# Triangular factors turned by VectorE block transposes instead of a trip through DRAM, with the first steps ordered anew

## The chip, the cores and the metric

The kernel runs on one core of one Trainium2 chip. Its metric is the device time of one execution in microseconds; three runs of the kernel before took 694.21 (median), 695.6 and 693.18 us.

Engines are named as in the profile: PE is TensorE (matrix products; PEld its weight loads), DVE is VectorE, ACT is ScalarE, POOL is GpSimd, and SP is the engine that issues most DMAs. Each engine works through its own list of instructions in order and waits where an operand isn't ready.

## The reference

A delta-rule attention layer is followed by a hard-swish MLP. Batch 4, 8 heads, 768 tokens, head width 48:

```python
k_n = k / (np.linalg.norm(k, axis=-1, keepdims=True) + 1e-06)
for t in range(S):
    y[:, :, t] = einsum('bhd,bhde->bhe', q[:, :, t], state)
    v_old = einsum('bhde,bhd->bhe', state, kt)
    state = state + bt * einsum('bhd,bhe->bhde', kt, vt - v_old)
...
x = y.transpose(0, 2, 1, 3).reshape(3072, 384)
h = x @ w_in                      # 384 x 2048
g = h * clip(h + 3, 0, 6) / 6
out = g @ w_out                   # 2048 x 384
```

q, k, v and beta are float32; the two weight matrices arrive as float64.

## The kernel before, in words

**Attention in chunks.** The tokens are cut into 24 chunks ("tiles" t) of 32 tokens; the 4 batches of a chunk fill the 128 partitions (partition = batch, token). Within a chunk the recurrence becomes linear algebra: with L the strictly lower triangular 32x32 matrix of beta-weighted key products of one batch and head, the chunk needs the inverse of (1 + L). There are 4 x 8 = 32 such matrices in a chunk.

- `prep(t)` normalizes the keys (POOL, kb), transposes keys and queries on PE (pt, copied by ACT to KQ), forms the scores (sc), and multiplies them with a mask on VectorE into LB. LB holds two halves for each head: the factor L, and the masked query-key scores.
- `lower(t)` sends the half with L to a DRAM scratch, l_dram, through SP (L446).
- Chunks come in groups: group 0 is chunk 0 alone, groups 1 to 5 have four chunks each, group 6 has three. A group of four has 4 x 32 = 128 matrices. `inverse(g)` loads them from l_dram with one matrix per partition (tile A, 1024 elements each), runs 30 pairs of VectorE instructions (a product pr, L719, and a subtraction from A, L724), sets the diagonal, stores A to x_dram (L730) and loads it back, chunk by chunk, over the L half of LB (L738).
- Group 1 is needed early. `halves_of(1)` does only the two 16x16 diagonal blocks, in 14 pairs (L681, L686), with the same trip out (L671) and back (L693, L700), and `join(t)` fills the remaining block with two sets of small PE products (pi, L633) between VectorE block transposes (L643, L651).
- Chunk 0 uses `product(0)`, a scheme of PE products and 32x32 VectorE transposes, with no DRAM.
- `chain(t)` is the recurrence: state times keys and queries (ks, L775), the right side R on VectorE (L788), the inverse times R on PE (pz, ACT copy Z), the state update (su, L892; VectorE L907), and the chunk's output y (py, yt, ACT copy xT).

**MLP.** Two chunks make a block of 256 tokens. `up` multiplies with w_in (ph, 16 column units of 128; L946). ACT computes relu(ph/6 + 1/2) into t1 (L955, three buffers), and VectorE min(t1, 1) * ph into g (L958). Block 0 is done in halves by chunk, ua and ub. `down` multiplies with w_out (po, L987); from block 2 on, `down_by_seven` does this with seven half-size products on sums of g (L1052; the sums on VectorE, L1038).

**Weights.** Sixteen pieces of 768 KB (w_in eight, w_out eight) are loaded in float64 (L310) and turned to float32: four ACT instructions for the exponent (L335, word `a`), three VectorE instructions (L357, L362, L368, word `c`). Their raw data lie in `spare` and in parts of w_out.

**What sets the order.** The schedule is written by hand. Until the fifth chunk it is the string ORDER: each word advances one generator by a step, and the engines' instruction lists follow from it. `k`, `q`, `v`, `w` issue loads on SP; `pN`, `nN`, `mN`, `bN` are parts of prep of chunk N; `i1`, `i2` are steps of the inverse of group 1 and 2; `x` is product or join; `h` and `y` the chain and its output; `ua`, `ub`, `u` MLP units with their ACT part (`ra`, `rb`, `ru`) and VectorE part (`ga`, `gb`, `gu`). From chunk 5 on a loop over chunks does it: 15 MLP units a chunk, with chain and prep steps at fixed units, and the steps of the next group's inverse as fill from the second chunk of each group. SP allows about eight DMAs in flight: each issue waits for the landing of the eighth before it.

Of the kernel before, what the change touches and what calls it, by code (L numbers as in the profile page):

```python
# [9 lines left out]
FP32 = mybir.dt.float32  # L10
# [5 lines left out]
ALU = mybir.AluOpType  # L16
# [6 lines left out]
k*4 B*4 w s n0 k*2 n0 z*2 s k n0*2 z n0 k z n1 n0*2 q z a*3 p0 m0 k*2 q n1*2 q c k q s c n1 w p0 a  # L23
p0*3 k a k n2 k*2 q z s k*2 q p0 w n1*2 a c n1 p0 s q a p1 x0 n2*2 a n2 s x0 n2 x0*2 k a n2 a*2
n2*2 p1 n2 q*3 a m1 c w k x0*2 c q s k c x0 b0 p1 a q p1 a p2 v x0 c p1 a c x0 c*3 v q x0 n4*2 p2
k x0 p2*2 p1 w b1 a b2 m2 c q n4 q*3 p2 q c*2 p1 v x0 w n4*3 p3 a*2 n4 p2 m3 p3 a*2 q p3 p4 x0 a w
p3 p4 a p2 c p3 q p4 x0 p4*2 a*3 m4 v p3 a k c p4 p3 p4 w c*2 a c x0*2 h0 a c a l1 l2 a c l3 h0 l4
a*2 c y0 i1 k y0 v b3 y0 c*2 k y0 w ua*2 w i1 ra i1*4 ua i1*7 a i1 k i1*7 a i1*2 k v ra i1*2 a ga
i1 h0 i1 ra ua i1 ua i1 ra i1 ga ua ga*2 ra c ga ra k ga h0 ua ra ga k ua n5 a ra v ga ua a ra c
ua v ra i1 ga*2 c a ua h1 ua*2 n5 x1 w ra*2 ua ga i1 x1 ga c x1 v k x1 x2 k x1 n5 ra n5 i1 ga a*2  # L30
h1 x1 c m5 w ua c v h1 ra y1 h1 x3 y1*2 a h1 ga i1 k*2 a v c a*2 h1 y1 ua ra a n5 x2 k h2 y1 k x2
n5 b4 c y1 ga ub*2 ra k ga q k n5 x2 w ub rb n5 a n5 v n5 k rb x2 gb y2 n5*2 gb rb x2 q ub rb n5
h2 ub gb rb i1 q gb p5 gb k p6 s h2 v ub rb k p5 h2 p5 ub x3*2 q y2 q k v b5 b6 x4 x3 gb k n9 q
ub*3 rb w rb*2 gb*2 c a v gb ub y2 ub k y2 h2 rb gb rb gb v rb a*2 v n9 gb h2 x3*2 ub p5 q rb ub c
ub p5 p7 gb y2 ub rb*2 h3 gb*2 c v p6 a k a y2 h3 p8 k y3 p6 k rb gb k n9 u q y3 p7 h3 q k n9 p7
h3 p8*2 a c k q y3*2 p6 c y3 u y3 a p6 c m6 w q u c a ru h3 a n9 gu x4 h3 a u k q ru q k c q*2 a v
k q a u q u gu n9 p5 v c k p6 a p7 w p7 u n9 p6 ru p5 v*2 n9 m7 v b8 a gu u p8 n9 p8 m8 p7 c p8 q
ru p7 n9 s u a p8 u b7 q u l5 a gu k u n9 a u ru n9*2 v c gu q u p9*2 c h4 ru c gu q l6 a p9 c*3 v
x4*2 u l8 ru h4 u p10 gu l7 y4 k m9 m10 y4 p10 q u q p10 q u i2*2 ru i2*4 k gu p10 x4 p10 v x4 p9
i2 p9 i2 q u*2 i2 v i2*2 v i2*2 ru i2*4 k i2*3 gu i2 u h4 i2*2 ru i2*4 p9 h4 p9 p10*2 i2 u*2 k gu  # L40
ru u*2 i2*3 q i2 gu i2*4 k u i2 u i2 ru gu u b10 u i2 ru i2*9 q ru k u gu u l10 e h4 e y4 u i2*2
gu i2*2 k i2 ru i2 l9 i2 q i2 ru i2 u i2 u i2*3 k i2 k b9 k p11 h4 k y4 k*4 e i2 y4 gu e i2*3 u*2
gu y4
# [4 lines left out]
def kernel(  # L48
# [368 lines left out]
    l_dram, x_dram = {}, {}  # L417
# [13 lines left out]
    def scaled(t):  # L431
        needs(("kb", t), *pad(t), *([("bkb", t - NKB)] if t >= NKB else []))
        nc.gpsimd.tensor_tensor(
            out=bkbufs[t % NBKB][:, :, 0:D], in0=kbufs[t % NKB][:, :, 0:D],
            in1=beta_tok[:, t, 0:H].unsqueeze(2).to_broadcast([P, H, D]), op=ALU.mult,
        )
        past.add(("bkb", t))
        yield

    def lower(t, dma=nc.sync):  # L440
        g, i = group(t)
        if g > 0:
            if g not in l_dram:
                l_dram[g] = scratch.tile([size(g), H, P, C], FP32, name=f"l_dram{g}")
                x_dram[g] = scratch.tile([size(g), H, P, C], FP32, name=f"x_dram{g}")
            dma.dma_start(  # L446
                out=l_dram[g][i].rearrange("h p c -> p h c"),
                in_=LBs[t][:].rearrange("p e a j w -> p (e a) j w")[:, :, 0, :],
            )
        past.add(("L", t))  # L450
        yield

    def prep(t, whole=True):
# [36 lines left out]
        for p in range(NP):  # L490
# [12 lines left out]
        LB = work.tile([P, 2, NP, 2, C], FP32, name="LB", bufs=NLB)  # L503
        mb = mbs.pop(t)
        nc.vector.tensor_tensor(  # L505
            out=LB[:].rearrange("p e a j w -> p e (a j w)"), in0=sc[:, :, 0 : NP * 2 * C],
            in1=mb[:].rearrange("p e a j w -> p e (a j w)"), op=ALU.mult,
        )
# [5 lines left out]
        if whole:  # L514
            drain(lower(t))
            yield

    def product(t):
# [7 lines left out]
        LT = LBs[t][:].rearrange("p e a j w -> p (e a) j w")[:, :, 0, :]  # L526
# [88 lines left out]
    def join(t):  # L615
# [6 lines left out]
        LT = LBs[t][:].rearrange("p e a j w -> p (e a) j w")[:, :, 0, :]  # L622
# [41 lines left out]
    def halves_of(g):  # L664

        n = size(g) * H * B
        needs(*(("L", first(g) + i) for i in range(size(g))))
        At = work.tile([128, C + 1, C], FP32, name="A", bufs=1)
        flat = At[0:n].rearrange("p c i -> p (c i)")
        A = flat[:, 0 : C * C]  # L670
        nc.sync.dma_start(  # L671
            out=A, in_=l_dram[g][:].rearrange("t h (b c) i -> (t h b) (c i)", b=B),
        )
# [3 lines left out]
        for j in range(1, HC - 1):  # L677
# [15 lines left out]
        nc.sync.dma_start(  # L693
            out=x_dram[g][:].rearrange("t h (b c) i -> (t h b) (c i)", b=B), in_=A,
        )
        past.add(("out", g))
        for i in range(size(g)):
            yield
            LBv = LBs[first(g) + i][:].rearrange("p e a j w -> p (e a) j w")
            nc.sync.dma_start(out=LBv[:, :, 0, :], in_=x_dram[g][i].rearrange("h p c -> p h c"))  # L700
            past.add(("halves", first(g) + i))
# [631 lines left out]
```

## Time and profile before

| | |
|---|---|
| median of 3 runs | 694.21 us |
| the profiled execution | 691.84 us, span 690.1 us |
| PE busy | 648.2 us (94%) |
| VectorE busy | 440.1 us (64%) |
| ScalarE busy | 239.8 us (35%) |
| mean granted PE clock | 0.975 |
| DMA moved | 45.27 MB |
| l_dram, x_dram transfers | 23 of 128 KB out (2.7 us each), 6 to A (5.1), 6 from A (3.6), 23 of 128 KB back (4.0) |

The profile follows one execution. A line of a timeline has start, duration, engine, source line, operation and operands, and in brackets the idle time before it and what ended that. A line of the table of stretches has the stretch, its length, busy time with the count of instructions for each engine asked for, the mean granted PE clock, the DMA share and GB/s. The chain is the line of work that ended last, followed back from the end.

### The profile page before, as it was taken

What the parts mean: (1) busy time and instruction counts of PE and PEld (TensorE: products, weight loads), DVE (VectorE), ACT (ScalarE), POOL (GpSimd) and SP (SyncE); (2) the same over time, 40 slices, a digit from 0 to 9 for tenths busy, and PEclk for the clock granted to TensorE, in tenths of its full rate; (3) what the DMA queues carried; (4) which work ended last, traced back from release to release, by engine and by line L of the source; (5) the groups of instructions that cost most, each with busy time, mean ns of one, the idle gap of its engine ahead of it and who ended that gap; (6) DMA issues with size and microseconds to landing.
All of it is one profiled execution on the core that took longest, in us unless ns stands there. A gap on an engine that the chain in (4) does not pass through costs nothing.

```text
span 690.1 us, 25473 instructions
## 1 busy us (share of the span) xinstructions
PE 648.2 (94%) x11208; PEld 568.0 (82%) x11208; DVE 440.1 (64%) x1174; ACT 239.8 (35%) x476; POOL 95.2 (14%) x146
## 2 busy tenths in 40 slices
PE   1659799999999999999999999999999999999997
PEld 1548687767678988988988988988988989989997
DVE  5878656788535985834985734984544984445242
ACT  5886558522133223232233232232222132132230
POOL 5440021710401100501100401100000000000000
PEclk9967799999999999999999999999999999999999
DMA  7987746513614126024025122025020014000000
GB/s 163 211 205 212 167 99 145 111 21 92 74 36 97 22 47 91 14 47 95 15 47 77 28 47 64 10 48 82 10 70 2 2 36 59 24 3 1 25 0 24
DMA packets 137999, 45.27 MB, mean 66 GB/s; under 512 B 128192, under 2 KB 131264, under 8 KB 137888
## 3 DMA queue, kind: packets, MB, share of 16 engines
q1 hardware_dynamic: 137632, 43.35, 30.6%
q8 instruction: 88, 1.44, 0.9%
q10 hardware_dynamic: 256, 0.30, 0.2%
q14 instruction: 23, 0.19, 0.1%
HBM read 32.87 MB, written 10.75 MB: 63 GB/s over the span
## 4 chain that ended last, share of the span: by engine, by line
PE 78%; DVE 11%; DMA 6%; issue 2%; ACT 2%; SPq 1%; DVEq 0%
PE ph L946 33%; PE po L1052 23%; PE po L987 6%; PE ks L775 3%; PE pz L796 3%; PE py L796 3%; PE su L892 2%; DVE A L724 2%; PE pt L474 2%; DMA w_out<-in_moe_w_in_dram 2%; PE sc L495 2%; DVE pr L719 2%; DMA spare<-in_moe_w_in_dram 2%; DVE g L1038 1%; ACT spare L335 1%
## 5 line engine op out<-in xcount | busy, mean ns | idle before, releaser
L946 PE MATMUL ph<-xT,w_in 128*128 128x256 f32 (+1 forms) x1248 | 270.7, 370 | 2.7 <-DVE g L958 1.6
L946 PEld LDWEIGHTS ph<-xT,w_in 128*128 128x128 f32 x1248 | 221.2, 193 | 32.1 <-DVE g L958 2.6
L955 ACT ACTIVATE t<-ph,halves 128x256 f32<-128x256 f32 (+1 forms) x208 | 94.8, 457 | 203.8 <-PE ph L946 194.2
L958 DVE SCALAR_TENSOR_TENSOR g<-t,ph 128x256 f32<-128x256 f32 (+1 forms) x208 | 81.7, 397 | 124.6 <-ACT t L955 124.5
L1052 PE MATMUL po<-w_out,g 128*128 128x192 f32 x640 | 113.3, 328 | 0.0
L1052 PEld LDWEIGHTS po<-w_out,g 128*128 128x128 f32 x640 | 103.9, 190 | 0.5
L1052 PE MATMUL po<-spare,g 128*128 128x192 f32 x480 | 84.8, 330 | 0.0
L1052 PEld LDWEIGHTS po<-spare,g 128*128 128x128 f32 x480 | 78.1, 190 | 1.8
L1038 DVE TENSOR_TENSOR g<-g 128x256 f32<-128x256 f32 x160 | 65.5, 463 | 0.5 <-PE po L1052 0.5
L724 DVE TENSOR_TENSOR A<-A,pr 128x30 f32<-128x30 f32 (+19 forms) x150 | 52.1, 348 | 3.5
L335 ACT ACTIVATE spare<-spare,places 128x768 uint16<-128x768 uint16 (+1 forms) x56 | 52.3, 939 | 1.9 <-DMA spare<-in_moe_w_in_dram 1.0
L719 DVE TENSOR_TENSOR pr<-A 128x30 f32<-128x30 f32 (+19 forms) x150 | 50.4, 336 | 3.3
L423 POOL TENSOR_TENSOR mb<-beta_tok,mask 128x256 f32<-128x256 f32 x48 | 35.2, 755 | 78.3 <-DVE LB L505 78.3
L987 PE MATMUL po<-w_out,g 128*128 128x384 f32 x128 | 44.8, 490 | 0.0
L1059 ACT ACTIVATE o<-po 128x192 f32<-128x192 f32 x40 | 13.2, 330 | 88.6 <-PE po L1052 84.3
L458 POOL TENSOR_TENSOR kb<-kf,inv 128x384 f32<-128x384 f32 x24 | 21.8, 910 | 147.0 <-PE pt L474 88.8
L482 ACT ACTIVATE KQ<-pt 128x512 f32<-128x512 f32 x48 | 28.3, 594 | 30.5 <-PE pt L474 29.7
L845 ACT ACTIVATE xT<-yt 128x384 f32<-128x384 f32 x24 | 11.7, 486 | 68.6 <-PE yt L841 68.6
L987 PEld LDWEIGHTS po<-w_out,g 128*128 128x128 f32 x128 | 23.4, 190 | 13.4 <-issue 0.6
L907 DVE TENSOR_TENSOR state<-state,su 128x384 f32<-128x384 f32 x46 | 23.3, 547 | 14.7 <-PE su L892 14.7
L775 PEld LDWEIGHTS ks<-state,KQ 64*64 64x64 f32 x1472 | 24.2, 138 | 6.2 <-issue 5.7
L788 DVE SCALAR_TENSOR_TENSOR y<-ks,parity,y 128x192 f32<-128x192 f32 x46 | 17.0, 410 | 18.4 <-ACT y L812 18.3
(104 smaller groups left out, 570.3 us busy)
## 6 DMA issues: line engine op xcount, KB each, us to landing
kf<-in_k_dram SPq DMA_DIRECT2D x96, 48.0 KB, 2.6
qb<-in_q_dram SPq DMA_DIRECT2D x96, 48.0 KB, 2.9
vf<-in_v_dram SPq DMA_DIRECT2D x96, 48.0 KB, 3.2
out_dram<-o SPq DMA_DIRECT2D x92, 48.0 KB, 1.6
spare<-in_moe_w_in_dram SPq DMA_DIRECT2D x4, 768.0 KB, 7.6
w_out<-in_moe_w_in_dram SPq DMA_DIRECT2D x4, 768.0 KB, 6.9
w_out<-in_moe_w_out_dram SPq DMA_DIRECT2D x4, 768.0 KB, 7.8
spare<-in_moe_w_out_dram SPq DMA_DIRECT2D x4, 768.0 KB, 5.5
```

The costliest lines, as they stand in the source:

```text
L335: nc.scalar.activation(out=z, in_=z if n else d.bitcast(I16)[:, :, :, 3], func=func, bias=places[:, n : n + 1], scale=scale,)
L423: nc.gpsimd.tensor_tensor(out=mb[:, e], in0=beta_tok[:, t, e:H:2].unsqueeze(2).unsqueeze(3).to_broadcast([P, NP, 2, C]), in1=mask2[:].unsq ...
L719: nc.vector.tensor_tensor(out=pv, in0=A[:, j, j + 1 :].unsqueeze(1).to_broadcast([n, j, w]), in1=A[:, 0:j, j].unsqueeze(2).to_broadcast([n ...
L724: nc.vector.tensor_tensor(out=A[:, 0:j, j + 1 :], in0=A[:, 0:j, j + 1 :], in1=pv, op=ALU.subtract)
L775: nc.tensor.matmul(ph[y][c, e, D * p : D * p + D], lhsT=KQ[r, p * B // 2 + b // 2, 2 * y : 2 * y + 2, :].rearrange("k y c -> k (y c)"), rh ...
L796: nc.tensor.matmul(ps[rows(place(b)), D * h : D * h + D], lhsT=m(h)[rows(b)], rhs=z[rows(b), D * h : D * h + D], start=True, stop=True, sk ...
L946: nc.tensor.matmul(ph[:, cols], lhsT=w_in[:, s, f * 128 : (f + 1) * 128], rhs=xT[:, s, cols], start=(s == 0), stop=(s == NKT - 1),)
L955: nc.scalar.activation(out=t1, in_=ph, func=ACTF.Relu, bias=half, scale=1.0 / 6.0)
L958: nc.vector.scalar_tensor_tensor(out=g, in0=t1, scalar=1.0, in1=ph, op0=ALU.min, op1=ALU.mult)
L987: nc.tensor.matmul(pos[c][:], lhsT=gs[blk, f // 2][:, f % 2, c * P : (c + 1) * P], rhs=w_out[:, f, :], start=(f == 0), stop=(f == NFC - 1),)
L1038: nc.vector.tensor_tensor(out=A(f, *out), in0=A(f, *a), in1=A(f, *b), op=op)
L1052: nc.tensor.matmul(ps[n][:], lhsT=A(f - f % 2, *a)[:, f % 2], rhs=b[:, f], start=(f == 0), stop=(f == HF - 1),)
```

## The change

Four edits:

- The factors no longer go through DRAM. prep writes L into a tile of its own, `L` (four chunks), and the scores into a smaller LB, with two VectorE instructions in place of one. `taken(g)` transposes L in 32x32 blocks into A, one matrix per partition, and `given(g)` transposes A back into a tile `X`, which pz, `product` and `join` read. Each is one VectorE instruction of 128x1024; both of its operands step by 32 elements. `lower`, l_dram, x_dram and their DMAs are gone. Chunk 0 writes L directly into its X.
- ORDER is a new string. Up to its end it does the same steps apart from those that no longer exist (the words l1 to l10, four of i1, four of i2).
- ACT writes its part of the hard-swish into g itself, and VectorE finishes it in place; t1 is gone.
- The steps of a last group with three chunks run on all 128 partitions, the rest filled with zeros.

```diff
 ORDER = """
-k*4 B*4 w s n0 k*2 n0 z*2 s k n0*2 z n0 k z n1 n0*2 q z a*3 p0 m0 k*2 q n1*2 q c k q s c n1 w p0 a
+k*3 B k B*3 z n0*3 w z*3 s z q*2 n0 q n0 q v n0 w n0 a p0 a p0 s p0*2 m0 k*2 w p0 a*3 p0 a c a c v
...
 """
...
+    def inverted(g):
+        if g not in Xs:
+            if g >= 2:
+                needs(*(("pz", first(g - 2) + i) for i in range(size(g - 2))))
+            Xs[g] = work.tile([P, GS, H, C], FP32, name="X", bufs=2)
+        return Xs[g]
+
+    def lowers(t):
+        g, i = group(t)
+        if g == 0:
+            return inverted(g)[:, i]
+        if g not in Ls:
+            needs(*([("A", g - 1)] if g >= 2 else []))
+            Ls[g] = work.tile([P, GS, H, C], FP32, name="L", bufs=1)
+            if size(g) < GS:
+                nc.gpsimd.memset(Ls[g][:, size(g) :], 0.0)
+        return Ls[g][:, i]
...
+    def turn(x):
+        return x[:].rearrange("p t h i -> p i (t h)")
+
+    def problems(A):
+        return A.rearrange("p (c i) -> p i c", i=C)
+
+    def taken(g, A):
+        nc.vector.transpose(out=problems(A), in_=turn(Ls[g]))
+        past.add(("A", g))
+
+    def given(g, A):
+        nc.vector.transpose(out=turn(inverted(g)), in_=problems(A))
...
-    def lower(t, dma=nc.sync):
-        g, i = group(t)
-        if g > 0:
...
-            dma.dma_start(
-                out=l_dram[g][i].rearrange("h p c -> p h c"),
-                in_=LBs[t][:].rearrange("p e a j w -> p (e a) j w")[:, :, 0, :],
-            )
...
-        LB = work.tile([P, 2, NP, 2, C], FP32, name="LB", bufs=NLB)
+        LB = work.tile([P, H, C], FP32, name="LB", bufs=NLB)
         mb = mbs.pop(t)
-        nc.vector.tensor_tensor(
-            out=LB[:].rearrange("p e a j w -> p e (a j w)"), in0=sc[:, :, 0 : NP * 2 * C],
-            in1=mb[:].rearrange("p e a j w -> p e (a j w)"), op=ALU.mult,
-        )
+        for j, out in enumerate((lowers(t), LB)):
+            nc.vector.tensor_tensor(
+                out=out.rearrange("p (e a) w -> p e a w", e=2), in0=scv[:, :, :, j, :],
+                in1=mb[:, :, :, j, :], op=ALU.mult,
+            )
...
-        dma.dma_start(
-            out=A.rearrange("p c i -> p (c i)"),
-            in_=l_dram[g][:].rearrange("t h (b c) i -> (t h b) (c i)", b=B),
-        )
+        taken(g, flat)
...
-        back.dma_start(
-            out=x_dram[g][:].rearrange("t h (b c) i -> (t h b) (c i)", b=B),
-            in_=A.rearrange("p c i -> p (c i)"),
-        )
-        past.add(("out", g))
-        for i in range(size(g)):
-            yield
-            LBv = LBs[first(g) + i][:].rearrange("p e a j w -> p (e a) j w")
-            back.dma_start(out=LBv[:, :, 0, :], in_=x_dram[g][i].rearrange("h p c -> p h c"))
-            past.add(("X", first(g) + i))
+        given(g, flat)
+        past.update(("X", first(g) + i) for i in range(size(g)))
...
-        of_heads(pz, lambda b: b, lambda h: LBv[:, he(h), 0, :], R)
+        of_heads(pz, lambda b: b, lambda h: X(t)[:, he(h), :], R)
+        past.add(("pz", t))
...
-                t1 = mlp.tile([128, TB], FP32, name="t1", bufs=3)[:, cols]
-                nc.scalar.activation(out=t1, in_=ph, func=ACTF.Relu, bias=half, scale=1.0 / 6.0)
+                nc.scalar.activation(out=g, in_=ph, func=ACTF.Relu, bias=half, scale=1.0 / 6.0)
...
-                        out=g, in0=t1, scalar=1.0, in1=ph, op0=ALU.min, op1=ALU.mult
+                        out=g, in0=g, scalar=1.0, in1=ph, op0=ALU.min, op1=ALU.mult
```

`halves_of(1)` changes in the same way as `inverse` (shown), with `taken` in place of its load and `given` in place of its store and loads.

In the instruction lists that follow from the new ORDER: on SP the eighth w_in piece is the 43rd transfer instead of the 54th. On PE the first state update su of chunk 0 stands ahead of the first up-projection ph, as do all scores sc of chunks 1 to 4; fifteen up-projections with ks of chunk 1 (fourteen before) stand ahead of the first join product. On ACT all 32 conversion instructions of w_in stand ahead of the last three KQ copies of chunks 3 and 4. On VectorE the 28 factor steps of group 1 stand behind the conversions of w_in, as before, with twelve instead of four hard-swish instructions among them. Group 2's factor steps lie between MLP units 17 and 36 of the u stream; before, between 18 and 36, with the last chain steps of chunk 4 among them.

## The prediction

> **What bounds the kernel now.** I read the page's first two parts, then engine busy time by stretch, the chain, the waits ahead of ScalarE's weight work, and VectorE in one dense stretch. From the page:
>
> ```profile
> span 690.1 us, 25473 instructions
> PE 648.2 (94%) x11208; PEld 568.0 (82%) x11208; DVE 440.1 (64%) x1174; ACT 239.8 (35%) x476; POOL 95.2 (14%) x146
> ...
> PE   1659799999999999999999999999999999999997
> ...
> PEclk9967799999999999999999999999999999999999
> ```
>
> TensorE is full from the sixth slice on. Busy time of PE in stretches of the span (start:end, length, busy, granted clock, DMA share, GB/s):
>
> ```profile
> 40.00:54.40 14.40, 7.64 (x327) 0.58 0.78 201
> 54.40:61.30 6.90, 6.89 (x94) 0.63 0.53 142
> 61.30:72.30 11.00, 9.01 (x248) 1.00 0.88 240
> 72.30:84.00 11.70, 9.45 (x277) 0.56 0.77 151
> 84.00:100.00 16.00, 15.18 (x519) 1.00 0.54 119
> ...
> 230.00:690.00 460.00, 454.81 (x7011) 1.00 0.20 37
> ```
>
> From 230 us on PE lacks 5.2 us, of which 3.6 lie after 650, in the unchanged tail: 1.6 us is all that later stages could give. PE's work before and after is the same, so the time moves by what PE idles, or runs at half clock, before 184 us, and by new stalls later. The chain, in time order (start, length):
>
> ```profile
> 52.53 0.96 DVE w_in L368
> ...
> 61.30 3.56 DMA x_dram<-A
> 64.88 4.55 DMA LB<-x_dram
> ```
>
> The trip back costs 3.56 + 4.55 = 8.1 us. The trip out costs nothing: group 1's factor steps begin at 53.41, right behind that weight conversion, with A issued at 47.95. Up to 52.5 the chain is ScalarE's conversions. Their waits for weights:
>
> ```profile
> 15.76 0.99 ACT L335 ACTIVATE spare<-spare,places 128x768 uint16<-128x768 int16 x1 [0.97 <-DMA spare<-in_moe_w_in_dram]
> 21.33 1.00 ACT L335 ACTIVATE spare<-w_out,places 128x768 uint16<-128x768 int16 x1 [0.23 <-DMA w_out<-in_moe_w_in_dram]
> 26.83 0.99 ACT L335 ACTIVATE spare<-w_out,places 128x768 uint16<-128x768 int16 x1 [1.11 <-DMA w_out<-in_moe_w_in_dram]
> 33.21 1.04 ACT L335 ACTIVATE spare<-w_out,places 128x768 uint16<-128x768 int16 x1 [0.45 <-DMA w_out<-in_moe_w_in_dram]
> ```
>
> Sum 2.76 us. Last, VectorE where a later group is factored, and after it:
>
> ```profile
> 228.00:256.00 28.00, 26.92 (x73) 1.00 0.19 38
> 256.00:268.00 12.00, 8.73 (x29) 1.00 0.25 66
> ```
>
> VectorE has 1.1 us free in 28; PE stalls 0.58 us for it at 255. Behind that, 3.3 us are free in 12.
>
> **What the skill says.** The Trainium skill, "TensorE: Matmul & The Clock Gate", Part 1: the array falls to half clock after an idle window of some 3.4 us and comes back after a busy one. The trace agrees in kind: PE is half idle from 68 to 72, and from 74 to 82 the clock is 0.50. "Vector Engine (DVE) Microarchitecture Reference", section 5.2: about 1.04 ns a column, but near 2.0 when source and destination both hop at every element, up to 2.5 for small steps. The trace has no such transpose. "DMA: Bandwidth & Descriptors", Anatomy of one DMA: about 2 us of a transfer are fixed (given for the path from GpSimd), mostly the write receipt; the 128 KB loads here, issued by SP, take 4.0 us in all.
>
> **The change, part by part.**
>
> *DMAs.* 23 + 23 transfers of 128 KB and 6 + 6 of up to 512 KB go, and their queue slots. SP waits 95.3 us for LB behind L446, but PE waits for nothing queued there after 60 us, so beyond the 8.1 us I count nothing. If loads were late, PE would show it; its one wait for a load is 1.8 us at 41.6.
>
> *Transposes.* Two a group, six groups, 128x1024. Contiguous ones took 0.44 us at 256 columns and 0.978 at 768: 1.05 ns a column, so 1.25 us at 1024. Here both sides step by 32 words. Below: 1.25; above: 1024 x 2.5 + 0.16 = 2.7 (skill). A reduction reading at that step took 0.314 us for 128 elements, against 0.29 at the slope of the contiguous one; writing is unseen. I take 2.2.
>
> *LB in two halves.* One 0.684 us instruction becomes two of 256 columns. At 0.42 each (the same shape at L569), +0.16 us a tile.
>
> *t1 removed.* ScalarE writes g itself. Same instructions; g's previous readers stand earlier on PE than the matmuls it evicts, so no new wait. Nothing, on either side under 0.5 us.
>
> *Order, to the first up-projection.* In SP's new queue the eighth w_in piece has 35 small loads ahead of it instead of 46, the second comes 11th instead of 17th. A piece landing blocks the eighth transfer behind it (the waits at 15.76 and 21.32 end as a piece lands), so pieces arrive earlier. ScalarE has the same 38.5 us between 8.3 and the copy xT that ends at 54.36: 7.5 us idle. Walking its new list with the trace's durations I find 1.2 us idle before the first conversion, 1.3 at the first KQ copies and some 2.5 scattered: xT ends near 51.9. **-2.5 us**, about the four waits above. Bounds: 0 (VectorE's product chain holds ScalarE) and -5.
>
> *Order, from there to the other half block (first ub).* Tile 4's last KQ copy now comes after all conversions, at 50.8; its scores take 1.0 to 51.9, two LB halves to 52.8, the first transpose to 55.0. The 28 factor steps took 7.7 us (53.41 to 61.2); 12 instead of 4 g's stand among them, 0.2 each as they overlap: 65.1. PE's twelfth up-projection is no earlier (half clock first, 1.4 us each as at 54.4, then 0.77). Second transpose to 67.3, two 0.44 us turns, the first join matmuls at 68.4 instead of 69.95. Thus the trip's 8.1 us go, but the steps start 2.1 us later against the first up-projection, hold 1.6 us more g's and 2.2 us of transpose. Then join (0.4, 0.3 and 0.45 on VectorE, 0.4), R after two other instructions (72.0), pz 0.85, Z 0.5, py 0.85, y 0.6, yt 0.4, pi 0.4, xT 0.5: ub starts at 75.9. The kernel before starts it at 84.69 with su and ks done (0.85 + 1.1 at full clock): comparable 77.9, 6.8 us sooner, if the clock stays up. From 66.7 to 75.9 PE has about 4.5 us of work, less than before, so I expect it to fall again: what ran at 0.5 then lost 4.2 us (9.45 busy x 0.44). I charge 2.9, weighing it at 0.7. Start to ub: **-3.9 us**, the first -2.5 included.
>
> *84 to 184 us.* Before idles 4.3 us here. Two waits of PE for join operands (0.71, 0.95) go, as all four tiles' factors arrive together; in their place chain 3 has one 0.75 us up-projection and 0.4 us of join between ks and pz, while R needs 1.5: about 1.2 more with its yt. Group 2's steps are packed in 20 units instead of being spread; VectorE is over nine tenths busy in both. **-0.5**, bounds -3 and +3.
>
> *Steady loop.* The first transpose stands where the DMA was issued (sixth unit of a group's second tile), 6 units ahead of the dense stretch, so it hides in VectorE's idle time. The dense stretch has a split LB. The second transpose follows the last factor step, soon followed by the state update: 2.2 + 1.0 us in which up-projection g's queue. Four PSUM buffers of 1.3 us each cover about 3. If the cover fails each costs up to 1 us. I take 0.2 a group, five groups: **+1.0**, bounds 0 and +6.
>
> Sum: -3.9 - 0.5 + 1.0 = -3.4. The profiled execution, 691.84 us (span 690.1 and 1.74 around it), becomes 688.4. It lies 2.4 under the median 694.21; the same shift there gives **690.8**. 0.3% is 2.1 us, about what a measurement here tells from no change.
>
> **Rivals.**
> 1. *The clock stays up* (0.20). Without the charge of 2.9 us the sum is -6.3: 687.9. For it: the window is free-running by the skill's account, and PE's gaps here are under 2 us each. Against: the same stage fell before.
> 2. *Nothing is left* (0.20). ScalarE keeps its idle time because its KQ copies wait for PE and POOL, the clock falls fully, the trip back was merely exchanged for later steps: start -1, steady +1: 694.2.
> 3. *VectorE becomes the bound of the loop* (0.18). Each transpose at 2.7 us or above stands in front of g's and the state update and stalls PE by a microsecond at both places: 10 x 1.0 = 10 us against 4.4 gained: 700. It decides from 0.44 us a transpose. For it: 26.92 of 28 busy. Against: both sit outside the dense stretch, and ks comes 6.5 us after the state update.
>
> **How the numbers follow.** My forecast (0.42) has its own range, 688 to 693. Faster: nearly all of forecast and rival 1, 0.60. Same: rival 2 mostly, 0.21. Slower: 0.19. The range reaches from 683.5 (rival 1 with both low bounds, -2.5 each, would be 682.9) to 699 (most of rival 3).
>
> **What would show it.** First ph on PE near 52 (right within 1.5 us); ScalarE waits for weights under 1 us; the two transposes 1.25 to 2.7 us; the first join near 68; a clock under 0.7 between 70 and 82 (rival 1: none); PE idle from 230 on at most 7 us (rival 3: over 12). I am wrong if first ph does not move, or if VectorE waits appear ahead of PE in the loop.

## The result, and the profile after

The changed kernel takes 690.60 us (median of 14 runs, 688.93 to 692.36); the kernel before, beside it on the same chip, 694.11 us (14 runs, 691.62 to 696.40). The ratio is 0.9954, 95% interval 0.9940 to 0.9968: some 3.2 us faster. The forecast was 690.8.

The profiled executions differ by less: 691.84 us before, 690.61 after. The profile of before is one of its quicker executions, the profile of after lies at its median. A second profile of before, taken later (696.02 us), is therefore read beside the first.

The page of the changed kernel, span, busy times, and the slices of PE and its clock:

```profile
span 688.9 us, 25309 instructions
PE 644.7 (94%) x11208; PEld 565.0 (82%) x11208; DVE 464.3 (67%) x1210; ACT 239.1 (35%) x476; POOL 92.9 (13%) x147
...
PE   1468799999999999999999999999999999999997
...
PEclk9999799999999999999999999999999999999999
```

PE's busy time fell by 3.5 us, as less of the same work ran at half clock (mean granted clock 0.990, before 0.975), but its idle time grew from 41.9 to 44.2. VectorE has 24.2 us more; twelve transpositions of 2.08 to 2.10 us alone are 25.1. The stretches shown of before, now in the changed kernel (start:end length, PE busy, clock, DMA share, GB/s):

```profile
40.00:54.40 14.40, 11.29 (x378) 0.88 0.81 224
54.40:61.30 6.90, 5.67 (x48) 1.00 0.83 235
61.30:72.30 11.00, 8.19 (x252) 0.92 0.47 83
72.30:84.00 11.70, 9.46 (x325) 0.65 0.02 4
84.00:100.00 16.00, 15.94 (x483) 1.00 0.20 59
230.00:690.00 460.00, 452.95 (x6999) 1.00 0.10 22
```

PE is denser from 40 to 54 us (11.29 busy, 7.64 before) and the first up-projections run at full clock. From 72 to 84 us the clock is low again, as before. From 84 to 100 PE now idles 0.06 us (0.82). From 230 us to the end of the span it lacks 5.9 us (5.2). Three points of this stage on PE, before and then after: the first up-projection, the join, and the first up-projection of the other half block (ub):

```profile
54.41 4.21 PE L946 MATMUL ph<-xT,w_in 128*128 128x128 f32 x18 [0.58 <-ACT xT L845]
...
69.95 0.73 PE L633 MATMUL pi<-LB,VY 16*32 16x16 f32 x64 [0.91 <-DVE VY L643]
...
84.69 2.27 PE L946 MATMUL ph<-xT,w_in 128*128 128x128 f32 x18
```

```profile
55.19 2.94 PE L948 MATMUL ph<-xT,w_in 128*128 128x128 f32 x24 [0.58 <-ACT xT L846]
...
69.54 1.39 PE L654 MATMUL pi<-X,VY 16*32 16x16 f32 x128 [1.85 <-DVE VY L664]
...
80.44 2.72 PE L948 MATMUL ph<-xT,w_in 128*128 128x128 f32 x12
```

The chain, where it had the trip back through DRAM (start, length):

```profile
55.03 2.03 DVE A L448
58.78 3.62 PE ph L948 x30
66.92 2.10 DVE X L452
```

The 8.1 us of the two DMAs have become 2.1 us. But the first transposition starts at 54.95, because L of the group's last tile is written at 54.3 to 54.7; in the first profile of before it was written at 44.2 to 44.9. The new order has handed most of the saved trip to other work ahead of it. ScalarE's waits up to its copy of xT:

```profile
10.15 1.94 ACT L335 ACTIVATE spare<-spare,places 128x768 uint16<-128x768 int16 x2 [3.35 <-DVE places L252]
13.22 0.60 ACT L504 ACTIVATE KQ<-pt 128x512 f32<-128x512 f32 x1 [1.12 <-PE pt L496]
...
54.65 0.49 ACT L846 ACTIVATE xT<-yt 128x384 f32<-128x384 f32 x1 [1.24 <-PE yt L842]
```

No wait for a weight load is left (2.76 us before); waits for VectorE and PE stand in their place. VectorE in the dense stretch (226.2 to 254.2 us, shifted by the 1.8 us that the loop now runs ahead) is busy for 26.57 of 28 us, about as before (26.92).

**A kind of idle time that the prediction did not count.** The profile marks a wait "issue" where an engine sat idle and no engine, buffer or load that the profile shows released it. PE has such waits. First the kernel before, up to 184 us, three of six, 5.65 us in all:

```profile
46.08 0.44 PE L545 MATMUL pi<-VY 32*32 32x32 f32 x17 [1.15 <-issue]
...
75.55 1.18 PE L796 MATMUL pz<-R,LB 32*32 32x48 f32 x47 [1.54 <-issue]
...
100.88 0.24 PE L633 MATMUL pi<-LB,VY 32*32 32x16 f32 x6 [0.95 <-issue]
```

The changed kernel has three, 2.60 us:

```profile
37.26 1.17 PE L797 MATMUL pz<-vf,X 32*32 32x48 f32 x44 [0.98 <-issue]
...
47.39 0.99 PE L517 MATMUL sc<-KQ 64*32 64x64 f32 x68 [0.64 <-issue]
...
73.25 0.88 PE L654 MATMUL pi<-X,VY 32*32 32x16 f32 x50 [0.98 <-issue]
```

The second profile of before has eight, 7.26 us. So 3.1 to 4.7 us of this kind are gone, where the profiled times fell by 1.2 and 5.4 us. The experiments come back to it.

The same executions, cut at the first ks of tile 5, where the steady loop begins (us):

| kernel | ks of tile 5 | from there to the span's end |
|---|---|---|
| before, first profile | 174.01 | 516.1 |
| before, second profile | 178.25 | 516.1 |
| changed | 171.05 | 517.9 |
| changed, tile 0's norm first (experiment 4) | 170.30 | 518.1 |
| and group 4's norms late (6) | 168.40 | 516.7 |
| and fillers (9) | 166.22 | 516.6 |
| changed code, order of before (11) | 175.79 | 517.0 |
| the same, two loads later (12) | 172.94 | 516.7 |

All that was gained was gained before 171 us, and 1.8 us of it was given back later.

### The profile page after: what moved, and what is told of

It is laid out like the page before. It is cut to its first block, busy times and chain, and to the rows that moved or that the text cites. A ratio compares the mean times of both kernels' runs of the same rounds, so it can differ in the third digit from the quotient of the medians.

```text
span 688.9 us, 25309 instructions
## 1 busy us (share of the span) xinstructions
PE 644.7 (94%) x11208; PEld 565.0 (82%) x11208; DVE 464.3 (67%) x1210; ACT 239.1 (35%) x476; POOL 92.9 (13%) x147
## 4 chain that ended last, share of the span: by engine, by line
PE 76%; DVE 14%; DMA 4%; issue 2%; SPq 2%; ACT 1%; POOL 0%; DVEq 0%; ACTq 0%
PE ph L948 33%; PE po L1053 21%; PE po L988 5%; PE ks L776 3%; PE pz L797 3%; DVE A L734 3%; PE pt L496 3%; PE su L894 2%; PE py L797 2%; DVE pr L729 2%; DVE g L1039 2%; PE sc L517 2%; DMA vf<-in_v_dram 1%; PE yt L842 1%; DVE R L789 1%
## 5 line engine op out<-in xcount | busy, mean ns | idle before, releaser
L956 ACT ACTIVATE g<-ph,halves 128x256 f32<-128x256 f32 (+1 forms) x208 | 94.8, 457 | 201.7 <-PE ph L948 200.9
L959 DVE SCALAR_TENSOR_TENSOR g<-g,ph 128x256 f32<-128x256 f32 (+1 forms) x208 | 81.0, 396 | 106.0 <-ACT g L956 105.8
L1053 PEld LDWEIGHTS po<-w_out,g 128*128 128x128 f32 x640 | 103.8, 190 | 0.5
L734 DVE TENSOR_TENSOR A<-A,pr 128x30 f32<-128x30 f32 (+9 forms) x150 | 54.2, 361 | 3.7
L729 DVE TENSOR_TENSOR pr<-A 128x30 f32<-128x30 f32 (+9 forms) x150 | 50.3, 335 | 3.0
L458 POOL TENSOR_TENSOR mb<-beta_tok,mask 128x256 f32<-128x256 f32 x48 | 34.5, 741 | 47.2 <-DVE LB L528 47.1
L496 PE MATMUL pt<-ident,kb 128*128 128x128 f32 x96 | 16.2, 295 | 14.7 <-POOL kb L480 14.5
```

The lines of the kernel that those rows point to most:

```text
L458: nc.gpsimd.tensor_tensor(out=mb[:, e], in0=beta_tok[:, t, e:H:2].unsqueeze(2).unsqueeze(3).to_broadcast([P, NP, 2, C]), in1=mask2[:].unsq ...
L496: nc.tensor.transpose(pt[:, p, :], src[:, 2 * p : 2 * p + 2].rearrange("p e w -> p (e w)"), ident[:])
L729: nc.vector.tensor_tensor(out=pv, in0=A[:, j, j + 1 :].unsqueeze(1).to_broadcast([n, j, w]), in1=A[:, 0:j, j].unsqueeze(2).to_broadcast([n ...
L734: nc.vector.tensor_tensor(out=A[:, 0:j, j + 1 :], in0=A[:, 0:j, j + 1 :], in1=pv, op=ALU.subtract)
L956: nc.scalar.activation(out=g, in_=ph, func=ACTF.Relu, bias=half, scale=1.0 / 6.0)
L959: nc.vector.scalar_tensor_tensor(out=g, in0=g, scalar=1.0, in1=ph, op0=ALU.min, op1=ALU.mult)
```

## Experiments

There are twelve, of which 10 and 11 are a kernel once more for a second profile. Ratios are to the kernel before on the same chip, and "over the changed kernel" is worked out from them, with the changed kernel at 0.9954.

### The code without the order, and the order without the code (1, 2, 11, 12)

Experiment 1 is the changed kernel with the old ORDER, its l words left out.

```diff
-k*3 B k B*3 z n0*3 w z*3 s z q*2 n0 q n0 q v n0 w n0 a p0 ...
+k*4 B*4 w s n0 k*2 n0 z*2 s k n0*2 z n0 k z n1 n0*2 q z a*3 p0 ...
```

> The changed kernel's code (block transposes, two half multiplies a tile, g in place) under the order of the kernel before, its ten store steps left out. Theory A (order and transposes pay only together: the new order spends some 10 us of the saved trip on making L of tiles 1 to 4 later): L complete near 45 us, taken near 48, given near 65.5, but the join stands behind ua in TensorE's order, so it cannot start before about 69; the conversions behind taken are 2.1 us later; time within 2 us of before, 692 to 696, so slower than the changed kernel by 2 to 5. Theory B (the saved trip alone is the gain): as fast as the changed kernel or better, 688 to 691. Theory C (the gain is the order's alone): 694 to 695, with no sign of the transposes.

Measured: 695.35 us, ratio 1.0003 (0.9992 to 1.0014). Nothing is gained, the number of theory A. Experiment 2 is the kernel before with the new ORDER.

```diff
-k*4 B*4 w s n0 k*2 n0 z*2 s k n0*2 z n0 k z n1 n0*2 q z a*3 p0 ...
+k*3 B k B*3 z n0*3 w z*3 s z q*2 n0 q n0 q v n0 w n0 a p0 ...
```

The words l1 to l10 stand behind their tile's last p, and four more i1 behind the last one, for the loads back.

> The kernel before with its trip through DRAM, under the new order, the ten stores put directly behind the tile's last step of prep and the four loads back behind the outgoing store. Theory A: L of the first group is complete near 55 us, A lands some 8 us later, near 63, the loads back some 8 us after the last step, so the join is near 79 to 82 where the changed kernel has 69.5; 8 to 11 us over the changed kernel, 698 to 702. Theory B: the same sign, since the trip is still there, but under 4 us over before. Theory C (the gain is the order's alone): 690 to 692, as the changed kernel.

Measured: 714.46 us, ratio 1.0290 (1.0259 to 1.0321), over twice the loss that theory A named. The profile (720.36 us) is the slowest of its six runs. VectorE in this kernel shows both legs of the trip:

```profile
64.70 0.19 DVE L681 TENSOR_TENSOR pr<-A 128x28 f32<-128x28 f32 x1 [7.79 <-DMA A<-l_dram]
...
84.38 0.77 DVE L643 STREAM_TRANSPOSE VY<-LB 128x256 f32<-128x256 f32 x2 [7.12 <-DMA LB<-x_dram]
```

Both waits hold everything that VectorE has queued behind them, the g's of the up-projections too: PE waits 3.82 us for a g at 66.4 us, and its join starts at 84.88, behind a 6.82 us wait for VectorE. The new order is a loss with the trip as it is placed here; other places for its stores and loads were not tried.

The profile of experiment 1 (701.3 us, the slowest of its 23 runs) has one "issue" wait of 4.12 us at 47 us. A second profile was taken.

> The changed kernel's code under the order of before once more, for a second profile: the first was 6 us over the median of that kernel's runs, with one idle stretch of 4.12 us at 47 us that no engine released. Theory A: L of tiles 1 to 4 complete near 45 us, the transposition back near 66 to 68, join near 70 to 72; as late as in before, since the conversions behind the first transposition, and with them the first up-projection, are 2 us later.

It took 694.48 us, with the same wait, longer. PE, then SP:

```profile
50.73 0.44 PE L565 MATMUL pi<-VY 32*32 32x32 f32 x17 [5.10 <-issue]
...
57.48 3.78 PE L947 MATMUL ph<-xT,w_in 128*128 128x128 f32 x18 [0.58 <-ACT xT L845]
```

```profile
41.78 1.12 SPq L309 DMA_DIRECT2D w_out<-in_moe_w_out_dram  x2
```

SP in the kernel before, in the same stretch:

```profile
36.53 8.80 SPq L446 DMA_DIRECT2D l_dram<-LB  x4
47.95 0.34 SPq L671 DMA_DIRECT2D A<-l_dram  x1
...
49.81 0.95 SPq L310 DMA_DIRECT2D w_out<-in_moe_w_out_dram  x2
```

In the kernel before SP stood 8.8 us at the four stores, waiting for LB, and the two 768 KB loads of w_out behind them were issued at 49.81. Without the stores SP reaches them at 41.78. From 42 to 51 us the data queue (q1: packets, MB, share of the 16 transfer engines' time) then takes 100.9%, in the first profile of before 63.4%:

```profile
q1 hardware_dynamic: 3359, 2.39, 100.9%
```

```profile
q1 hardware_dynamic: 4514, 1.19, 63.4%
```

Nine of these waits of PE are set against the 16 KB packets on the profile's instruction queue, which start 3.4 to 13.6 us apart between 20 and 80 us:

| profile | wait ends | packet in the half microsecond from | from packet to the end of the wait |
|---|---|---|---|
| before | 46.08 | 43.5 | 2.1 to 2.6 |
| before | 75.55 | 72.5 | 2.5 to 3.1 |
| before, second | 48.66 | 45.5 | 2.7 to 3.2 |
| changed | 37.26 | 34.5 | 2.3 to 2.8 |
| changed | 47.39 | 44.5 | 2.4 to 2.9 |
| changed | 73.25 | 70.5 | 2.2 to 2.8 |
| experiment 1 | 51.43 | 48.5 | 2.4 to 2.9 |
| experiment 11 | 50.73 | 47.5 | 2.7 to 3.2 |
| experiment 12 | 46.62 | 44.0 | 2.1 to 2.6 |

One match would say little. All fourteen traces together have 59 such waits up to 184 us; by their packet records 58 of them end 2.2 to 3.1 us after the start of a packet (the other, in experiment 2, 4.7 us). So PE very likely waits there for its own instructions. That they come late because loads fill the transfer engines is not shown: in experiment 6, which keeps the new order, the data queue takes 103.8% in the same stretch, and PE has no such wait from 36 to 69 us. The trace names no releaser, so this stays argued; what can be tried is the loads. Experiment 12 is experiment 1 with the two loads put on ScalarE's queue, in front of Z of tile 0.

```diff
-... x0*2 h0 a c a*2 c h0 a*2 c y0 i1 k y0 v b3 y0 c*2 k y0 w ua*2 w i1 ...
+... x0*2 h0 a c a*2 c w*2 h0 a*2 c y0 i1 k y0 v b3 y0 c*2 k y0 ua*2 i1 ...
-        nc.sync.dma_start(
+        (nc.scalar if i in (8, 9) else nc.sync).dma_start(
             out=raws[i].rearrange("p s f z -> p s (f z)"), in_=src.bitcast(U32)
```

> The changed kernel's code under the order of before, as in the two runs of that kind, but with the two 768 KB loads of w_out that SP there issues at 41.8 us moved to ScalarE's queue ahead of Z of tile 0, some 10 us later; in the kernel before, SP reached the first of them at 49.8 us, since it stood behind the stores of L. Contention theory: TensorE's idle stretch of 5.1 us at 46 us, which no engine released (1.15 and 1.51 us in two profiles of before), comes from its instructions arriving late while loads fill the transfer engines; with the loads away it is under 2 us, the first up-projection starts near 54.5 in place of 57.5 us, and the time is 1 to 2.5 us under before, 0.9965 to 0.9985. Rival (the stretch is not from these loads, or VectorE's first transposition holds the stage anyway): stretch as long as before or first up-projection not sooner, 0.9985 to 1.0015.

Measured: 692.24 us, ratio 0.9949 (0.9931 to 0.9967), a larger gain than the 0.9965 to 0.9985 that was expected. The kernel before, beside it, spread from 691.59 to 701.89 us. ScalarE issues the loads at 49.84. PE:

```profile
46.62 0.33 PE L565 MATMUL pi<-VY 32*32 32x32 f32 x17 [1.40 <-issue]
...
55.00 3.79 PE L947 MATMUL ph<-xT,w_in 128*128 128x128 f32 x18 [0.58 <-ACT xT L845]
```

The wait is 1.40 us and the first up-projection 2.5 us sooner than in experiment 11. The packet that ends the wait starts at 44.00 in place of 47.95. The gain passes down VectorE's queue: the transposition into A starts at 51.70 in place of 54.54, the one back at 68.24 in place of 71.05. With two loads held where the trip had held them by accident, the new code under the old order is as fast as the changed kernel, within the intervals. Theory A's number for experiment 1 was right and its reason wrong: the transpositions don't need the new order to pay.

The waits marked "issue" up to 184 us sum to 5.65 to 8.42 us in the four profiles of kernels with the trip (before twice, 2, 7), to 6.80 and 7.26 in experiments 1 and 11, and to at most 4.61 in the other eight.

### What a transposition costs in the steady loop (3, 8)

```diff
     def taken(g, A):
-        nc.vector.transpose(out=problems(A), in_=turn(Ls[g]))
+        for _ in range(3 if g > 2 else 1):
+            nc.vector.transpose(out=problems(A), in_=turn(Ls[g]))
```

and the same in `given`; experiment 8 has 2 in place of 3.

> The changed kernel with each of the two transpositions issued three times in groups 3 to 6, the result unchanged: 16 more instructions of 2.08 us, 33 us of VectorE in the steady loop. Theory A (hidden: between 230 and 650 us the changed kernel loses 1.9 us of TensorE in all): at most 2 us over the changed kernel, TensorE idle between 230 and 650 us under 4 us. Rival (VectorE nearly bounds the loop): a third or more of the 33 us shows, 700 us or above, TensorE idle above 12.

Measured: 715.65 us, ratio 1.0301 (1.0277 to 1.0325), 24 us over the changed kernel. The expectation (hidden) failed for three in a row. PE:

```profile
258.33 2.86 PE L950 MATMUL ph<-xT,w_in 128*128 128x256 f32 x12 [0.63 <-DVE g L961]
...
274.73 2.53 PE L950 MATMUL ph<-xT,w_in 128*128 128x256 f32 x6 [2.14 <-DVE g L961]
...
327.01 4.15 PE L950 MATMUL ph<-xT,w_in 128*128 128x256 f32 x18 [1.99 <-DVE g L961]
```

The first wait is in the kernel before too (0.58 us). The other two stand behind the three transpositions back (from A into X) and out (from L into A). After the one at 274.73 the clock fell (start:end length, PE, PEld, DVE, ACT and POOL busy, clock, DMA share, GB/s):

```profile
270.00:274.00 4.00, 2.58 (x12) 1.92 (x11) 3.93 (x3) 0.95 (x2) 0.00 (x0) 1.00 0.02 4
274.00:278.00 4.00, 3.27 (x10) 2.70 (x11) 2.93 (x8) 0.54 (x2) 0.00 (x0) 0.65 0.00 0
```

PE waits eight times in this way, 1.97 to 2.47 us, 16.8 us in all. In this profile (718.77 us, the slowest of its five runs) PE idles 16.6 us more than in the changed kernel's and is busy for 11.6 us more on the same work, which fits half clock after the waits. The clock did not fall each time: the 18 products at 327.01 above take 4.15 us, 0.23 each, where the six at 274.73 take 0.42 each. The Trainium skill, "TensorE: Matmul & The Clock Gate", Part 1, has the array fall to half clock after an idle window of some 3.4 us; here a wait of 2.14 us in an otherwise full stream was enough to see 0.65, so the measurement differs.

> The changed kernel with each transposition issued twice in groups 3 to 6: VectorE is then away 4.2 us in a row, not 6.3. Threshold theory (three in a row made TensorE wait 2.06 us each time, so 4.2 us are what the buffered products cover): waits of 0.2 us or less per pair, under 2 us over the changed kernel, 0.9954 to 0.9985 of before. Rival (every added microsecond of VectorE shows in proportion): half of what three in a row cost, 12 us over the changed kernel, 1.012.

Measured: 693.82 us, ratio 0.9990 (0.9973 to 1.0006): 2.5 us over the changed kernel, where "under 2" was expected and the rival said 12. The trace shows one wait more in the loop, 0.99 us at 215.2 behind the pair that begins at 209.6, and 0.35 to 0.4 us more in each later group (from su to ks around the pair back 11.6 us, in the changed kernel 11.2). So the first 8 added transpositions cost 2.5 us and the next 8 cost 22. There is a threshold, though not sharp at 4.2 us. The single transposition lies below it: from tile 5 on, 516.1 us became 516.7 in the profiles without the wait at 180 us (experiments 6 and 12), 0.6 us for the whole loop with all the edits in it.

### The late start, and a wait at 180 us (4, 6)

The new order puts the last four steps of tile 0's norm behind all settings in VectorE's queue (instructions that prepare constants), among them a transposition that waits for beta. Experiment 4 puts them in front.

```diff
-k*3 B k B*3 z n0*3 w z*3 s z q*2 n0 q n0 q v n0 w n0 a p0
+k*3 B k B*3 z n0*7 w z*3 s z q*4 v w a p0
```

> The changed kernel with tile 0's four last norm steps ahead of the settings in VectorE's order (and the q loads that stood between them four in a row as before). Theory A (the late start costs): the first transposition into PSUM starts near 8.7 us in place of 12.07; of these 3.4 us the chain of product(0), in which each step waits for another engine, carries some 2 to 3 us to its end near 38 us, but VectorE is full from 36 to 50 us, so that 0 to 2 us are left at the join: 688.5 to 690.6. Rival (VectorE's conversions set the first 55 us, the start is covered): first transposition 3.4 us sooner, join at 69.5 as now, 690.6 within 0.7.

Measured: 689.33 us, ratio 0.9917 (0.9900 to 0.9933), clear of the changed kernel's interval (0.9940 to 0.9968). PE:

```profile
8.66 1.12 PE L495 MATMUL pt<-ident,kb 128*128 128x128 f32 x4 [8.66 <-POOL kb L479]
...
52.90 2.94 PE L947 MATMUL ph<-xT,w_in 128*128 128x128 f32 x24 [0.58 <-ACT xT L845]
...
67.20 1.26 PE L653 MATMUL pi<-X,VY 16*32 16x16 f32 x128 [1.83 <-DVE VY L663]
```

Of 3.4 us at the first transposition 2.3 are left at the first up-projection and at the join, where the expectation saw 0 to 2. So VectorE's conversions do not cover the late start: tile 0's chain carries most of it to 55 us. In this profile the clock stayed at 0.50 from 70 to 82 us, and 0.75 us are left at tile 5; the medians' gain over the changed kernel, 2.6 us by the ratios, is larger than this profile explains.

In the changed kernel PE waits 1.03 us at 180 us for ScalarE:

```profile
180.27 0.86 PE L517 MATMUL sc<-KQ 64*32 64x64 f32 x64 [1.03 <-ACT y L813]
```

ScalarE itself had waited 4.12 us, up to 178.94, for VectorE's sums of group 4's norms (ss). Experiment 6 adds to experiment 4 that these norms begin later.

```diff
-                if i == 1 and 5 < u < 12:
+                if (i == 1 and 5 < u < 12) or (t == LS and u < 5):
                     continue
                 take(fill, 2 + (u % 3 == 0))
```

> Tile 0's norm first, and in the loop's first pass (tile 5) group 4's norms not begun before the sixth unit, so that VectorE's four reductions and their 0.94 us waits for POOL's squares do not stand between ks and R of tile 5. Theory: the 1.03 us for which TensorE waited at 180 us (scores behind y on ScalarE, whose queue held the root of these norms for 4.1 us) are gone and stay gone: 687.8 to 688.8, 0.9895 to 0.9910 of before. Rival (R stays late because of the transpose back at 169.7 and the quarter differences): 689.3 within 0.7, 0.9917.

Measured: 687.85 us, ratio 0.9899 (0.9880 to 0.9917). The wait is gone: PE has none between 140.3 and 250.4 us, and the stretch from tile 5 on is 516.7 us in place of 518.1. The intervals of 4 and 6 overlap, so the trace, not the ratio, carries this.

### The clock (5, 7, 9, 10)

Experiment 7 asks whether the half clock at the first up-projection was itself the cost in the kernel before. Fillers are products of the unit matrix (`spin`), overwritten by the real ones. One of the five places:

```diff
+    def spin(out):
+        nc.tensor.matmul(
+            out, lhsT=ident[:], rhs=ident[:], start=True, stop=True, skip_group_check=True
+        )
...
             ph = psM.tile([128, TB], FP32, name="ph", tag="pm")
+            for _ in range(3 if blk == 0 and f == 0 and half_of == 0 else 0):
+                spin(ph[:, cols])
```

> The kernel before with 32 fillers of the same kind in TensorE's idle stretches from 39.8 to 54.4 us (14 ahead of tile 4's q transposition, 7 ahead of pz, 5 of py, 3 of yt, 3 of the first up-projection). Theory A (the join sets the end of this stage): the clock at the first up-projection is 1.00 in place of 0.50 and its first 18 records take 2.2 us in place of 4.21, but the join still waits for the loads back, 69.45 to 69.95 us: 0 to 0.9 us are won, 0.9985 to 1.000 of before. Theory D (the half clock at the first up-projection is itself the cost, and its loss the changed kernel's gain): 2 us or more won, under 0.9970.

Measured: 695.37 us, ratio 0.9997 (0.9977 to 1.0018). PE:

```profile
55.88 2.27 PE L961 MATMUL ph<-xT,w_in 128*128 128x128 f32 x18
...
62.22 6.97 PE L961 MATMUL ph<-xT,w_in 128*128 128x128 f32 x42 [2.39 <-DVE g L973]
```

The 18 records take 2.27 us in place of 4.21, and PE then waits 2.39 us for VectorE. Nothing was won. The fillers cost twice their price, as each is two records of 0.12 us, so the first up-projection came 1.5 us later, and the 18 records end only 0.5 us sooner than before. The test is not clean: it shows that PE then waits for VectorE, not what full clock without fillers would give.

Experiment 10 is the kernel before, unchanged, for a second profile.

> The kernel before, unchanged, for a second profile, since the first was 2.4 us under the median of its runs. If the runs differ by how long TensorE sits in idle time that no other engine released (1.15, 0.95 and 1.54 us at 45, 71 and 74 us in the first profile), the second, if it is slower, has longer ones of these before 184 us and the same loop from 230 us on; if they differ by clock, it has more half-clock time and the same waits.

It took 696.02 us. PE in this second profile of the kernel before:

```profile
50.39 1.50 PE L796 MATMUL pz<-vf,LB 32*32 32x48 f32 x64 [1.29 <-DVE LB L605]
...
56.49 3.72 PE L946 MATMUL ph<-xT,w_in 128*128 128x128 f32 x18 [0.58 <-ACT xT L845]
...
72.07 0.73 PE L633 MATMUL pi<-LB,VY 16*32 16x16 f32 x64 [0.95 <-DVE VY L643]
```

It is 4.2 us slower with no more half clock at the first up-projection (3.72 us; 4.21 in the first profile). The join is 2.1 us later, "issue" waits are 7.26 us in place of 5.65, some of them longer and others shorter than in the first profile, and from tile 5 on both take 516.1 us. What differs between these two executions of the kernel before lies in front of the loop. The clock column of this profile reads 1.00 from 50 to 60 us, though pz took 1.50 us, against 0.88 at full clock elsewhere: the products' own durations are the safer reading.

Experiments 5 and 9 put fillers in front of the joins, py and yt of tile 1, on top of 4 and of 6.

```diff
             ps = psM.tile([P, H, HC], FP32, name="pi", tag="pm")
+            for _ in range({("pi1", 2): 7, ("pi2", 1): 3}.get((name, t), 0)):
+                spin(ps[:].rearrange("p h c -> p (h c)"))
```

This is experiment 9 ahead of the joins; experiment 5 has 13 and 7 there, both at tile 1.

> Tile 0's norm first (as in the run before), and 26 TensorE fillers whose results are overwritten: 128x128 products of the unit matrix by itself, some 0.12 us each at full clock, put in front of tile 1's two join products (13 and 7), its py (3) and yt (3), where TensorE idled 1.8, 0.9, 0.6 and 0.7 us. Clock theory: without idle the clock stays at 0.9 or more from 70 to 84 us, where 9 to 10 us of work ran at 0.5; the next up-projection half comes 2 to 4 us sooner and half of this lasts to the end: 686.5 to 688.5, or 0.9880 to 0.9905 of before. Rival (the clock falls whatever fills the gaps, or VectorE sets what follows): 0.9905 to 0.9930, as without fillers.

Measured: 694.64 us, ratio 0.9993 (0.9974 to 1.0012): a loss. Tile 2's product stands first in PE's order, so the fillers ran behind the wait, for 4.80 us. The clock was 1.00 from 72 us on, but the time was spent: 5.3 us over experiment 4.

> Norm first and late norms as in the run before, with 14 fillers of the same kind, each now priced by what the last fillers took (two matmul records of 0.12 us at full clock, so 0.25 us) and put where the idle time is: 7 in front of the first join product of the pair (tile 2's, which waits 1.83 us for VectorE's turn), 3 in front of tile 1's second (0.93 us), 2 before its py and 2 before its yt (0.6 and 0.7 us). Clock theory: the clock stays near 1.00 from 68 to 77 us, where it was 0.50 to 0.73; tile 1's chain up to the next up-projection half comes 1.5 to 3 us sooner, and some of it lasts: 686 to 687.2, 0.9870 to 0.9892 of before. Rival (the fillers cost what the clock gives, or it falls all the same): 0.9890 to 0.9915.

Measured: 684.46 us (four runs), ratio 0.9867 (0.9850 to 0.9883), 9.2 us under the kernel before, the best of all, and under both forecasts. Its interval still touches that of experiment 6. The clock part of the expectation did not come true (PE):

```profile
68.00:70.00 2.00, 1.91 (x72) 0.80 0.59 102
70.00:72.00 2.00, 2.00 (x54) 0.50 0.36 60
72.00:74.00 2.00, 1.39 (x51) 0.84 0.05 10
```

It fell all the same, for some 3 us, and the same products (the up-projection behind the join, pz) ran at half clock as in experiment 6. Of the 2.0 us by which the up-projection behind the join is sooner than in 6 (69.45 against 71.46), 0.76 were there at the first join product, 0.70 are an "issue" wait that is missing, and most of the rest is the second join product's clock (64 records in 0.80 us against 1.28). The 0.76 are not the fillers': the last up-projections ahead of the first filler already start 0.84 us sooner (60.31 against 61.15). Up to 184 us this profile has no "issue" wait at all. Whether the fillers do this, and what part of the 2.2 us by which tile 5 is sooner is theirs, was not separated.

## Why the prediction was right, and where it was not

The time, the sign and the range were right. The sum behind it was right in part only: it said 3.4 us against before's own profile, where 1.2 were found, and the median agrees because that profile was a quick one (against the second profile of before the gain is 5.4). That 690.8 fell so near 690.6 is luck.

- **Order, to the first up-projection (-2.5).** Failed. It starts at 55.19 us (54.41 and 56.49 in the two profiles of before). The waits for weights went, as said, but I took them for the bound. Tile 0's chain was most of it: its first product starts at 12.07 in place of 10.62, since the norm stands behind the settings, and experiment 4 moves the up-projection by moving that norm alone. The bound "0 (VectorE's product chain holds ScalarE)" was the case to take.
- **Transposes (2.2).** 2.08 to 2.10 us. The Trainium skill, "Vector Engine (DVE) Microarchitecture Reference", section 5.2, has 1.98 ns a column for a program with two sources in which all three ports hop at every element, which I read as source and destination; for a transposition it has no row. This trace gives 2.0, or 1.9 without the 0.16 us that I took as fixed.
- **LB in two halves.** 0.42 us each (median), as said. **t1**: no new wait shows; it was not tried alone.
- **Order, to the other half block (-3.9).** Join at 69.54, not 68.4; ub at 80.44 with su and ks to come, 82.4 on the scale on which before has 84.69: 2.3 us, not 3.9. The clock fell, as charged. Of the missing 1.6 us 1.1 were there at the join, and 0.5 came from there to ub. The first up-projection, 3.3 us later than forecast, cost less than that since it ran at full clock.
- **84 to 184 us (-0.5).** 0.7 us gained up to tile 5, then 1.03 lost at 180 us to group 4's norms. I had not followed ScalarE's queue there; experiment 6 removes it.
- **Steady loop (+1.0).** 0.6 us by experiments 6 and 12; in the changed kernel itself 1.8 with the wait at 180 us. Rival 3 (10 us) is refuted for single transpositions, and experiment 3 shows that it was one step away: at three in a row PE waits 2 us each time, and the loop loses 3.
- **DMAs ("beyond the 8.1 us I count nothing").** The step that failed most, unseen because it ran the other way in the sum. I looked for PE waiting for loads. What went beside the trip's own length was PE's "issue" waits (5.65 and 7.26 us before, 2.60 after), very likely for instructions; that the trip caused them is not shown, since experiments 1 and 11 have as much without it. What its stores gave was a hold on later loads, which experiment 12 shows. Each queue that a removed DMA stood in had to be followed for what moves up behind it.
- **Rivals.** The clock did not stay up (rival 1). "Nothing is left" (rival 2) has the time of experiment 1, the same code under the old order without two loads held back, though not its reason.

Still open: how much of the 3.2 us is the shorter stage and how much the "issue" waits. No run changes one alone in the changed kernel. Open too is why the crowded stretch of experiment 6 has no long wait.

## What to carry to other kernels

When a DMA leaves a queue, look at what stood behind it: its wait may have been holding large loads back, and by experiments 1 and 12 restoring the hold was worth 3.7 us by the ratios (3.1 by the medians). In a loop where the matrix engine is full, test the slack by repeating an instruction: one of 2.1 us cost next to nothing, three in a row cost 3 us a time. And profile the kernel before twice when the change is worth less than its spread.

## What was not expected of the hardware

- PE's waits marked "issue" ended 2.2 to 3.1 us after the start of a 16 KB packet on the instruction queue in 58 of 59 cases. One of them, ahead of the same product, took 1.15 and 1.51 us before, 1.40 in experiment 12, and 4.12 and 5.10 in experiments 1 and 11, where two 768 KB loads were issued 6 to 8 us earlier. A crowded data queue alone (103.8% in experiment 6) did not bring such a wait.
- A wait of 2.14 us in a full stream of matmuls was followed by a clock of 0.65 over the next 4 us; after one of 1.99 us (327.01) the products ran at full speed.
- A 128x128 float32 product of the unit matrix leaves two records of 0.12 us at full clock, 0.25 us in all.
